# The start-up of a one-core kernel: broadcast weights, an unbroken warm-up, and work moved between engines

## The chip, the cores and the metric

The kernel runs on one core of a Trainium2 chip. The metric is the device time of one execution in microseconds (us). The profile shows when each step of the start-up begins, to a hundredth of a microsecond.

The engines are TensorE (PE in the profile; PEld is its weight load), VectorE (DVE), ScalarE (ACT), GpSimd (POOL) and SyncE (SP, which only issues DMAs here).

## The reference

```python
# x: (8, 4096, 192) float32, weight: (8, 7), w_in: (192, 2048), w_out: (2048, 192), beta: (2048,)
w = exp(weight - weight.max(-1)); w = w / (w.sum(-1) + 1e-9)       # softmax over 7 taps, for each of 8 heads
y[b, s, h, g] = sum_k w[h, k] * x_pad[b, s + k, h, g]              # causal convolution, pad of 6
hid = y @ w_in                                                     # (32768, 2048)
out = (hid * sigmoid(beta * hid)) @ w_out                          # (32768, 192), float32
```

## The kernel before

The work is cut into 32 stages of 1024 tokens. A stage has 16 blocks of 128 hidden columns. A block is six matmuls into a PSUM tile `ph`, one SiLU on ScalarE that writes `g`, and "pairs" of output matmuls for earlier blocks. The convolution of later stages runs on VectorE. In stage 0 two thirds of the 192 columns run on TensorE, each third as seven matmuls with diagonal matrices `diag`, since nothing else is ready then; the last third is split between TensorE and VectorE. "Chunk 1's convolution" below is the first third of stage 1, done on TensorE from block 4 of stage 0 on. The change touches only the start-up and stage 0.

```python
    nc.scalar.dma_start(out=cw8, in_=weight)                 # 8 x 7, one row for each head
    load_x(x0, 0); load_x(x1, TOK); ...                      # SyncE's queue: x0, x1, w_out, ...
    load_w_in(0)                                             # GpSimd's queue, casts to bf16 on the way
    # softmax: exponential on 8 partitions, spread to 128 by a small matmul with a 0/1 matrix
    nc.vector.reduce_max(nmax, cw8, ...)
    nc.scalar.activation(e8[:, 0:K], cw8, AF.Exp, bias=nmax, accum_out=e8[:, K:K+1])
    nc.scalar.activation(warm, warm, AF.Silu)                # brings in ScalarE's SiLU table (1.28 us)
    fill(5)                                                  # matmuls on zeros, only to keep TensorE busy
    nc.tensor.matmul(pw, sel, e8, ...)                       # the small matmul
    fill(1, 384)
    for b in range(NB):
        cast_rows(nc.vector.tensor_copy, x0b, x0, b)         # x0 to bf16
    nc.vector.reciprocal(rn, pw[:, K:K+1]); nc.vector.tensor_scalar_mul(cw, pw[:, 0:K], rn)
    for b in range(NB):                                      # transposes of x0, evicted by ScalarE
        transposes(pt, x0b, b); nc.scalar.copy(tokens(xt0, b), pt)
        # fills of 256 and 384 columns after b = 0 and 1, then 384 and 256 behind the loop
    ... # diag = identity * cw, on VectorE
    for c in range(NG - 1):                                  # convolution of stage 0 on TensorE
        for k in range(K): diag_tap(k, xt0[:, c], pv[:, 0, :])
        nc.scalar.copy(cts[0][:, c, :], pv[:, 0, :])         # eviction
        for b in range(2): cast_rows(nc.scalar.copy, x1b, x1, 2 * c + b)
    ...
    scale_w_out(0)                                           # w_out times 1/beta, on VectorE
```

(Cuts are marked by `...`.)

## Time and profile before

| | before |
|---|---|
| time, median of the first 4 executions | 692.76 us (692.5 to 693.43) |
| transposes of x0 start | 4.76 us |
| first convolution on TensorE | 7.83 to 10.88 us |
| first SiLU | 14.31 us |
| second block of stage 1 | 33.01 us |
| end of the last eviction (ScalarE, 687.70 + 0.32) | 688.02 us |

After stage 0, TensorE is busy without a gap. These are the busy times by stretch of before: the stretch in us and its length, then busy time (and count) of TensorE, its weight loads, VectorE, ScalarE and GpSimd, the recorded clock, DMA share, GB/s.

```profile
16.40:31.90 15.50, 14.91 (x192) 9.02 (x192) 14.64 (x19) 15.06 (x15) 0.00 (x0) 1.00 0.92 203
31.90:679.00 647.10, 647.08 (x10881) 493.17 (x10881) 499.22 (x421) 551.86 (x496) 0.00 (x0) 1.00 0.35 92
```

TensorE has 0.02 us of idle in 647. With that code left as it is, only its start, its idle before that, and what follows its last matmul can change the total. (The trace of before holds no record of the clock, so the 1.00 in these lines says nothing about it; the step of the matmuls below does.) This is the start, from the timeline of before: start, duration, engine, line, operation, and in brackets the idle before it and what ended it.

```profile
1.26 2.31 PE L228 MATMUL ph<-zeros 128*128 128x512 bf16 x5 [1.26 <-DVE warm L178]
2.23 0.15 DVE L217 TENSOR_REDUCE nmax<-cw 8x1 f32<-8x7 f32 x1 [0.92 <-DMA cw<-in_weight_dram]
4.29 0.74 DVE L233 CAST x0b<-x 128x384 bf16<-128x384 f32 x2 [1.78 <-DMA x<-in_x_dram]
4.76 0.50 PE L240 MATMUL pb<-ident_b,x0b 128*128 128x128 bf16 x3
7.83 3.04 PE L279 MATMUL ph<-xt,diag 128*128 128x512 f32 x7
10.71 1.79 PE L279 MATMUL pb<-xt,diag 128*128 128x512 f32 x7
14.31 16.15 ACT L425 ACTIVATE g<-ph,beta 128x1024 bf16<-128x1024 f32 x15
```

The 8x7 weights are in at 2.2 us, before x0 (4.29). The seven matmuls of the first convolution start 0.43 us apart, those of the second 0.23 us: the step halves on the way, at about 10.5 us, and the text calls this the slow and the fast clock (in a_dve_order below the clock was recorded at 0.51 while the first convolution took 3.55 us). At the end of stage 0, TensorE waits for VectorE's last tap (from the timeline of before; the tap group ends at 29.27 + 2.60 = 31.87). The third line is the last eviction of the kernel:

```profile
29.27 2.60 DVE L335 SCALAR_TENSOR_TENSOR ct<-xt,cw,ct 128x1024 bf16<-128x1024 bf16 x2
31.92 0.61 PE L417 MATMUL ph<-ct,w_in_s 64*128 64x512 bf16 x4 [0.40 <-DVE ct L335]
687.70 0.32 ACT L466 COPY osb<-pa 128x192 f32<-128x192 f32 x1 [1.00 <-PE pa L450]
```

### The profile page before, as it was taken

The numbers are of one execution on the slowest core, as the hardware profiler recorded it, in microseconds if no ns is written. First come the engines' busy times: TensorE is split into PE (matmuls) and PEld (weight loads), VectorE is DVE, ScalarE is ACT, GpSimd is POOL, SyncE is SP. The second block draws the span as 40 slices with busy tenths as digits, with TensorE's granted clock in tenths as the row PEclk, the third lists the DMA queues.
The fourth block names the chain that finished last, engine by engine and source line by source line (L and its number), as shares of the span: only waits on it lengthen the run. The fifth ranks groups of instructions, "written<-read, shape, count | busy, mean of one in ns | idle before, by whom it ended". The sixth has DMA issues, their size and how long they took to land.

```text
span 690.7 us, 24335 instructions
## 1 busy us (share of the span) xinstructions
PE 684.2 (99%) x11311; PEld 518.1 (75%) x11311; DVE 526.6 (76%) x466; ACT 579.1 (84%) x531; POOL 6.8 (1%) x18
## 2 busy tenths in 40 slices
PE   8999999999999999999999999999999999999997
PEld 4677777777777777777777777777777777777776
DVE  6888877797777797777887777887777977777712
ACT  6988888888888888888888888888888888888883
POOL 3000000000000000000000000000000000000000
DMA  9754332344332343332344332443323443322111
GB/s 214 176 117 116 93 104 69 85 116 112 92 104 58 102 116 104 97 95 61 109 116 105 93 83 70 116 116 92 104 56 98 116 106 98 98 60 60 48 37 59
DMA packets 121445, 66.86 MB, mean 97 GB/s; under 512 B 53232, under 2 KB 121344, under 8 KB 121344
## 3 DMA queue, kind: packets, MB, share of 16 engines
q1 hardware_dynamic: 119632, 63.73, 34.7%
q0 software_dynamic: 1664, 1.57, 1.4%
q8 instruction: 88, 1.44, 0.9%
q14 instruction: 13, 0.11, 0.1%
q10 hardware_dynamic: 48, 0.01, 0.0%
HBM read 29.89 MB, written 25.17 MB: 80 GB/s over the span
## 4 chain that ended last, share of the span: by engine, by line
PE 97%; DVE 1%; ACT 1%; issue 0%; ACTq 0%
PE ph L417 47%; PE pa L450 24%; PE pb L450 24%; DVE ct L335 1%; ACT g L425 0%; PE ph L279 0%; ACT x1b L233 0%; DVE w_out_s L313 0%; PE pb L279 0%; PE ph L228 0%; DVE ct L396 0%; DVE xb L106 0%; ACT ct L326 0%; PE pb L240 0%; PE ph L240 0%
## 5 line engine op out<-in xcount | busy, mean ns | idle before, releaser
L425 ACT ACTIVATE g<-ph,beta 128x1024 bf16<-128x1024 f32 x512 | 569.7, 1114 | 95.7 <-PE ph L417 89.6
L450 PEld LDWEIGHTS <-g 64*128 64x128 bf16 x8160 | 367.7, 94 | 106.3 <-ACT g L425 0.7
L417 PE MATMUL ph<-ct,w_in_s 64*128 64x512 bf16 x3072 | 422.8, 376 | 1.3 <-ACT g L425 0.9
L335 DVE SCALAR_TENSOR_TENSOR ct<-xt,cw,ct 128x1536 bf16<-128x1536 bf16 (+2 forms) x190 | 336.6, 1772 | 2.5
L450 PE MATMUL pa<-w_out_s,g 64*128 64x192 bf16 x4112 | 244.2, 243 | 0.6 <-ACT g L425 0.5
L450 PE MATMUL pb<-w_out_s,g 64*128 64x192 bf16 (+1 forms) x4048 | 229.7, 243 | 0.0
L417 PEld LDWEIGHTS <-w_in_s 64*128 64x128 bf16 x3072 | 156.7, 94 | 56.7 <-issue 3.4
L468 DVE TENSOR_REDUCE osb<-pa 128x384 f32<-128x768 f32 x64 | 61.3, 957 | 120.8 <-PE pa L450 119.9
L468 DVE TENSOR_REDUCE osb<-pb 128x384 f32<-128x768 f32 x63 | 60.3, 958 | 28.9 <-PE pb L450 28.8
L106 DVE CAST xb<-xf 128x768 bf16<-128x768 f32 x60 | 40.5, 677 | 0.0
L333 DVE TENSOR_SCALAR ct<-xt,cw 128x1536 bf16<-128x1536 bf16 (+2 forms) x32 | 31.1, 972 | 0.0
L466 ACT COPY osb<-pb 128x192 f32<-128x192 f32 x1 | 0.3, 318 | 6.7 <-PE pb L450 6.7
L228 PE MATMUL ph<-zeros 128*128 128x512 bf16 (+2 forms) x10 | 4.7, 551 | 1.3 <-DVE warm L178 1.3
L210 POOL DMA_DIRECT2D w_in_s<-in_moe_w_in_dram x8 | 5.2, 653 | 0.0
L279 PE MATMUL pb<-xt,diag 64*128 64x512 f32 (+1 forms) x21 | 4.7, 453 | 0.0
L313 DVE TENSOR_TENSOR w_out_s<-w_out_raw,beta_r 128x768 bf16<-128x768 f32 x4 | 3.8, 956 | 0.7 <-DMA w_out_raw<-in_moe_w_out_dram 0.6
L121 DVE COPY xt<-xt 128x18 bf16<-128x18 bf16 x27 | 4.3, 159 | 0.0
L326 ACT CAST ct<-ph 128x512 bf16<-128x512 f32 x1 | 0.6, 586 | 3.3 <-PE ph L279 3.3
L279 PEld LDWEIGHTS pb<-xt,diag 64*128 64x128 f32 (+1 forms) x21 | 2.7, 187 | 0.7
L279 PE MATMUL ph<-xt,diag 128*128 128x512 f32 x7 | 3.0, 603 | 0.1
L233 DVE CAST x0b<-x 128x384 bf16<-128x384 f32 x4 | 1.5, 420 | 2.1 <-DMA x<-in_x_dram 2.1
L228 PEld LDWEIGHTS <-zeros 128*128 128x128 bf16 x10 | 1.2, 133 | 2.1 <-DVE warm L178 1.3
(51 smaller groups left out, 27.7 us busy)
## 6 DMA issues: line engine op xcount, KB each, us to landing
out_dram<-osb SPq DMA_DIRECT2D x127, 192.0 KB, 2.1
xf<-in_x_dram SPq DMA_DIRECT2D x60, 384.0 KB, 4.1
xt<-xb SPq DMA_TRANSPOSE x120, 3.1
x<-in_x_dram SPq DMA_DIRECT2D x4, 384.0 KB, 4.6
w_in_s<-in_moe_w_in_dram POOLq DMA_DIRECT2D x8, 192.0 KB, 9.8
w_out_raw<-in_moe_w_out_dram SPq DMA_DIRECT2D x4, 384.0 KB, 14.6
out_dram<-osb SPq DMA_DIRECT2D x2, 96.0 KB, 1.6
cw<-in_weight_dram ACTq DMA_DIRECT2D x1, 0.2 KB
```

Of the source, the lines that this page charges most:

```text
L106: nc.vector.tensor_copy(xbs[ch][:, :, :, h, :], xfs[ch][:, h].rearrange("q b (p c) -> q b c p", c=NG),)
L121: nc.vector.tensor_copy(dst, last[:, :, HALO + TOK - PAD :])
L210: nc.gpsimd.dma_start(out=w_in_s[r * DG : (r + 1) * DG, :, cols], in_=w_in_v[:, :, cols])
L228: nc.tensor.matmul(pf[:, 0, 0:cols], zeros[:, 0:128], zeros[:, 0:cols], start=True, stop=True)
L279: nc.tensor.matmul(pv, diag[rows, k, :], xt[rows, o : o + TOK], start=(k == k0), stop=(k == K - 1),)
L313: nc.vector.tensor_tensor(w_out_s[:, fcs, :], w_out_raw[:, fcs, :], beta_r[:, fcs].unsqueeze(2).to_broadcast((128, NQ, D)), ALU.mult,)
L333: nc.vector.tensor_scalar_mul(dst, src, scalar)
L335: nc.vector.scalar_tensor_tensor(out=dst, in0=src, scalar=scalar, in1=dst, op0=ALU.mult, op1=ALU.add)
L417: nc.tensor.matmul(ph[:, h, :], w_in_s[rows, j, fc * 128 : (fc + 1) * 128], cts[s][rows, j, :], start=(j == 0), stop=(j == NG - 1),)
L425: nc.scalar.activation(gs[s][:, fc], ph, AF.Silu, scale=beta[:, fc : fc + 1])
L450: nc.tensor.matmul(self.po[:, r, b * D : (b + 1) * D], g[rows, fc, self.h, q * BLK : (q + 1) * BLK], w_out_s[rows, fc, :], start=(self.don ...
L468: nc.vector.tensor_reduce(dst, self.po[:, :, 0 : nb * D].rearrange("p r n -> p n r"), axis=mybir.AxisListType.X, op=ALU.add,)
```

## The change

The intent is a shorter start-up. Its parts:
- The weights are loaded by DMA in broadcast form, one row for each of 128 partitions, so that the softmax needs no TensorE matmul.
- The warm-up fills are one unbroken run of nine, and the fills between the transposes are larger.
- The first 256 columns of w_in come raw over SyncE's queue and are cast by ScalarE, so GpSimd's software queue starts later (first issue at 7.67 us in the changed kernel, 2.17 before).
- Two x1 casts stand before ScalarE's first eviction.
- The first w_out scaling moves to GpSimd.
- Chunk 1's convolution is done in three blocks, not four, and three more output pairs are done in stage 0.

```diff
-    nc.scalar.dma_start(out=cw8, in_=weight)
+    for h in range(2):
+        nc.scalar.dma_start(out=wq[h * DG : (h + 1) * DG, :],
+                            in_=weight.unsqueeze(1).to_broadcast((H, HP, K)))
     load_x(x0, 0)
+    nc.sync.dma_start(out=beta_q, ...)
+    for r in range(2):
+        nc.sync.dma_start(out=w_in_raw[r * DG : (r + 1) * DG], in_=w_in_v[:, :, 0:F0])   # F0 = 256
     load_x(x1, TOK)
-    load_w_in(0)
-    nc.vector.reduce_max(nmax, cw8, ...)
-    nc.scalar.activation(e8[:, 0:K], cw8, AF.Exp, bias=nmax, accum_out=e8[:, K : K + 1])
+    nc.vector.reduce_max(nmax, wq, ...)
+    nc.scalar.activation(cw, wq, AF.Exp, bias=nmax, accum_out=total)
     nc.scalar.activation(warm, warm, AF.Silu)
+    nc.vector.reciprocal(total, total)
+    nc.vector.tensor_scalar_mul(cw, cw, total)
-    fill(5); nc.tensor.matmul(pw, sel, e8, ...); fill(1, 384)
+    fill(9)
     for b in range(NB):
         cast_rows(nc.vector.tensor_copy, x0b, x0, b)
+        if b == 1: diags(0, 2)
+    diags(2, 4); diags(4, K)
     for b in range(NB):
         transposes(pt, x0b, b); nc.scalar.copy(tokens(xt0, b), pt)
-        # fills of 256 and 384 after b = 0 and 1, 384 and 256 behind the loop
+        fill(1, (256, 384, 128, TOK)[b])          # and one of 512 behind the loop
+    nc.scalar.copy(w_in_s[:, :, 0:F0], w_in_raw)
     ...
+        for b in ((0, 1), (2,))[c]: cast_rows(nc.scalar.copy, x1b, x1, b)
         nc.scalar.copy(cts[0][:, c, :], pv[:, 0, :])
-        for b in range(2): cast_rows(nc.scalar.copy, x1b, x1, 2 * c + b)
+    cast_rows(nc.scalar.copy, x1b, x1, NB - 1)
     # scale_w_out(i): (nc.vector if i else nc.gpsimd).tensor_tensor(...)
-    CONV1 = {4: (0, 2), 5: (2, 4), 6: (4, 6), 7: (6, K)};  QUOTA_A = {3: 4, 7: 2};  last quota 8
+    CONV1 = {4: (0, 2), 5: (2, 4), 6: (4, K)};  QUOTA_A = {4: 2, 7: 5};  last quota 10
```

(The diff is cut to its core and some lines are joined. Cut are `+load_w_in(F0, FW)`, which loads the rest of w_in's first quarter later, the removal of the 0/1 matrix from GpSimd, a smaller tile of zeros for the fills, and an earlier warm exponential. The load of beta moves from ScalarE's queue to SyncE's.)

More of the change, by code (lines that the diff above doesn't have):

```diff
@@ L148, in load_w_out @@
         nc.sync.dma_start(out=w_out_raw[:, fcs, :], in_=w_out_v[:, fcs, :])
-    e8 = setup.tile([H, K + 1], FP32)
-    cw8 = setup.tile([H, K], FP32)
+    wq = setup.tile([128, K], FP32)
+    for h in range(2):
+        nc.scalar.dma_start(
+            out=wq[h * DG : (h + 1) * DG, :],
+            in_=weight.unsqueeze(1).to_broadcast((H, HP, K)),
+        )
     beta_q = setup.tile([NF, 128], FP32)
-    nc.scalar.dma_start(out=cw8, in_=weight)
-    nc.scalar.dma_start(out=beta_q, in_=moe_beta.rearrange("(c p) -> c p", p=128))
     def load_x(dst, t0):
@@ L167 @@
     load_x(x0, 0)
+    nc.sync.dma_start(out=beta_q, in_=moe_beta.rearrange("(c p) -> c p", p=128))
+    F0 = 256
+    w_in_raw = setup.tile([128, NG, F0], FP32)
+    for r in range(2):
+        nc.sync.dma_start(
+            out=w_in_raw[r * DG : (r + 1) * DG], in_=w_in_v[:, :, 0:F0]
+        )
     load_x(x1, TOK)
@@ L173 @@
     load(3)
-    zeros = setup.tile([128, TOK], BF16)
+    zeros = setup.tile([128, 128], BF16)
     nc.vector.memset(zeros, 0.0)
@@ L178, with load_w_in @@
     nc.vector.memset(warm, 0.0)
+    nc.scalar.activation(warm, warm, AF.Exp)
     xt0 = setup.tile([128, NG, HALO + TOK], FP32R)
     nc.vector.memset(xt0[:, :, 0:HALO].bitcast(FP32), 0.0)
-    nc.scalar.activation(warm, warm, AF.Exp)
-    sel = setup.tile([H, 2, DG], FP32)
-    nc.gpsimd.memset(sel, 1.0)
-    pattern = [[0, 2], [1, DG]]
-    nc.gpsimd.affine_select(
-        out=sel,
-        in_=sel,
-        compare_op=ALU.is_ge,
-        fill=0.0,
-        base=0,
-        pattern=pattern,
-        channel_multiplier=-HP,
-    )
-    nc.gpsimd.affine_select(
-        out=sel,
-        in_=sel,
-        compare_op=ALU.is_ge,
-        fill=0.0,
-        base=HP - 1,
-        pattern=[[-step, n] for step, n in pattern],
-        channel_multiplier=HP,
-    )
     ident = setup.tile([128, 128], FP32)
     make_identity(nc, ident)
-    def load_w_in(i):
-        cols = slice(i * FW, (i + 1) * FW)
+    def load_w_in(c0, c1):
         for r in range(2):
             nc.gpsimd.dma_start(
-                out=w_in_s[r * DG : (r + 1) * DG, :, cols], in_=w_in_v[:, :, cols]
+                out=w_in_s[r * DG : (r + 1) * DG, :, c0:c1], in_=w_in_v[:, :, c0:c1]
             )
-    load_w_in(0)
-    nmax = setup.tile([H, 1], FP32)
-    nc.vector.reduce_max(nmax, cw8, axis=mybir.AxisListType.X, negate=True)
-    nc.scalar.activation(
-        e8[:, 0:K], cw8, AF.Exp, bias=nmax, accum_out=e8[:, K : K + 1]
-    )
+    nmax = setup.tile([128, 1], FP32)
+    total = setup.tile([128, 1], FP32)
+    cw = consts.tile([128, K], FP32)
+    nc.vector.reduce_max(nmax, wq, axis=mybir.AxisListType.X, negate=True)
+    nc.scalar.activation(cw, wq, AF.Exp, bias=nmax, accum_out=total)
     nc.scalar.activation(warm, warm, AF.Silu)
@@ L226, in fill @@
     def fill(n, cols=TOK):
+        zc = zeros.unsqueeze(1).to_broadcast((128, cols // 128, 128))
         for _ in range(n):
-            nc.tensor.matmul(
-                pf[:, 0, 0:cols], zeros[:, 0:128], zeros[:, 0:cols], start=True, stop=True
-            )
+            nc.tensor.matmul(pf[:, 0, 0:cols], zeros, zc, start=True, stop=True)
     def cast_rows(copy, xb, x, b):
@@ L246, in tokens, with diags @@
         return xt[:, :, t : t + 2 * BLK].rearrange("p c (q b) -> p c b q", b=2)[:, :, b % 2]
+    nc.vector.reciprocal(total, total)
+    nc.vector.tensor_scalar_mul(cw, cw, total)
     beta = consts.tile([128, NF], FP32)
     beta_r = setup.tile([128, NF], FP32)
-    cw = consts.tile([128, K], FP32)
-    rn = setup.tile([128, 1], FP32)
-    fill(5)
-    pc = in_a()
-    pw, pb = pc[:, 0, 0 : K + 1], pc[:, 1, 0:NF]
-    nc.tensor.matmul(
-        pw, sel.rearrange("i h p -> i (h p)"), e8, start=True, stop=True
-    )
-    fill(1, 384)
+    diag = setup.tile([128, K, 128], FP32R)
+    def diags(k0, k1):
+        nc.vector.tensor_tensor(
+            diag[:, k0:k1],
+            ident.unsqueeze(1).to_broadcast((128, k1 - k0, 128)),
+            cw[:, k0:k1].unsqueeze(2).to_broadcast((128, k1 - k0, 128)),
+            ALU.mult,
+        )
+    fill(9)
     for b in range(NB):
         cast_rows(nc.vector.tensor_copy, x0b, x0, b)
-    nc.vector.reciprocal(rn, pw[:, K : K + 1])
-    nc.vector.tensor_scalar_mul(cw, pw[:, 0:K], rn)
+        if b == 1:
+            diags(0, 2)
+    diags(2, 4)
+    diags(4, K)
     hold = setup.tile([1, 1], BF16)
     nc.gpsimd.tensor_copy(hold, x0b[0:1, 0, 0, 0, 0:1])
+    load_w_in(F0, FW)
     for i in range(1, NW):
-        load_w_in(i)
-    diag = setup.tile([128, K, 128], FP32R)
+        load_w_in(i * FW, (i + 1) * FW)
     xt1 = setup.tile([128, HALO + TOK], FP32R)
@@ L294 @@
         nc.scalar.copy(tokens(xt0, b), pt)
-        if b == 0:
-            fill(1, 256)
-        elif b == 1:
-            fill(1, 384)
-    fill(1, 384)
+        fill(1, (256, 384, 128, TOK)[b])
+    pb = in_a()[:, 0, 0:NF]
     nc.tensor.transpose(pb, beta_q, ident[0:NF, 0:NF])
     nc.scalar.copy(beta, pb)
-    fill(1, 256)
-    for k0, k1 in ((0, 3), (3, K)):
-        nc.vector.tensor_tensor(
-            diag[:, k0:k1],
-            ident.unsqueeze(1).to_broadcast((128, k1 - k0, 128)),
-            cw[:, k0:k1].unsqueeze(2).to_broadcast((128, k1 - k0, 128)),
-            ALU.mult,
-        )
+    fill(1)
+    nc.scalar.copy(w_in_s[:, :, 0:F0], w_in_raw)
     def scale_w_out(i):
         fcs = slice(i * NQ, (i + 1) * NQ)
-        nc.vector.tensor_tensor(
+        (nc.vector if i else nc.gpsimd).tensor_tensor(
             w_out_s[:, fcs, :],
@@ L325 @@
             diag_tap(k, xt0[:, c], pv[:, 0, :])
+        for b in ((0, 1), (2,))[c]:
+            cast_rows(nc.scalar.copy, x1b, x1, b)
         nc.scalar.copy(cts[0][:, c, :], pv[:, 0, :])
-        for b in range(2):
-            cast_rows(nc.scalar.copy, x1b, x1, 2 * c + b)
+    cast_rows(nc.scalar.copy, x1b, x1, NB - 1)
     def tap(dst, src, k):
@@ L377, in second @@
         nc.vector.tensor_copy(xt1[:, HALO - PAD :], xt[:, 0, HALO - PAD :])
-    CONV1 = {4: (0, 2), 5: (2, 4), 6: (4, 6), 7: (6, K)}
+    CONV1 = {4: (0, 2), 5: (2, 4), 6: (4, K)}
     conv1_ps = []
@@ L523 @@
         5: [None],
-        7: [conv1_evac, lambda: scale_w_out(2), lambda: rows_of(2), None],
+        6: [conv1_evac, lambda: scale_w_out(2), lambda: rows_of(2), None],
         8: [None, lambda: scale_w_out(3)],
@@ L528 @@
     }
-    QUOTA_A = {3: 4, 7: 2}
+    QUOTA_A = {4: 2, 7: 5}
     queue = deque()
@@ L545 @@
             elif u > 7:
-                output(s, u, 5 if u < NF - 1 else 8, "ab")
+                output(s, u, 5 if u < NF - 1 else 10, "ab")
             elif u in QUOTA_A:
```

## The prediction

> **What bounds the kernel now.** Busy time by stretch: from 31.9 to 679.0 us of the 690.7 us span TensorE is busy 647.08 of 647.1 us. A block of hidden columns costs 1.31 us there (starts 33.01, 34.32, 35.63 in the timeline), ScalarE's SiLU only 1.11. The change leaves that code alone, so only the first 32 us and TensorE's idle in it can move. There the chain of waits runs:
> - Warm-up and transposes to 7.8 us.
> - First convolution 7.83-10.88: seven matmuls, 0.43 us from start to start; from about 10.5 us the step is 0.23.
> - ScalarE 10.90-14.31: two evictions (0.59, 0.58) and four casts (0.66 each) in a row. First SiLU at 14.31.
> - Stage 0: 16 SiLUs at 1.08 us. TensorE idles 0.75 us before 15.47.
> - VectorE without a gap 22.33-31.88, ending in taps which TensorE waits for (resumes 31.92).
>
> **What the change does.**
> 1. Warm-up. Nine fills (0.43 us cold, estimate 3.9) run from about 1.1 to 5.0 us, and larger fills stand between the transposes. [...] after the broken warm-up the step halves only at 10.5 us, after 2.7 us of dense convolution. I give 65% that convolution 0 is already fast: 7 x 0.23 = 1.6 instead of 3.0 us.
> 2. ScalarE order. It gains a 128x768 cast of w_in (estimate 0.9 us from 0.59 for 512 columns), but two x1 casts now precede the first eviction and run under the convolution. From the beta copy's end at about 7.7: 0.9 + 4 x 0.66 + 2 x 0.58 = 4.7, plus handover: first SiLU at 12.8 us (13.9 if the clock is late), 1.5 earlier.
> 3. DMA. Before, x1's second half lands 8.3 us after issue, at about 10.6, sharing the engines with w_in's software queue. That queue now starts later, and x1 should land by 8.5 although 0.39 MB of raw w_in goes ahead of it.
> 4. Softmax. No TensorE matmul; the weights should land by about 3.3 us and cw be ready near 4.3, when x lands. x0 casts stay about where they are (4.3 to 6.1-6.6).
> 5. VectorE. The first w_out scaling (0.96 us) goes to GpSimd, removing a 0.62 us DMA wait; the second-chunk evictions (15.33 before) start near 13.1. Chunk 1's convolution ends one block earlier. So VectorE's last tap ends near 29.8 instead of 31.88. The GpSimd scaling should [...] be ready for the first output matmul, now at block 4.
> 6. Quotas: 52 instead of 49 output pairs in stage 0: at 0.082 us a pair, 0.25 us.
>
> **Sum.** TensorE resumes for stage 1 about 2.0 us earlier with 0.25 less left: 2.2 us if warm, about 1.1 if not. Everything after is the same dense sequence. I predict 691.0 us, 690.1 to 692.3. Faster by 2% would need 13.9 us out of a start-up of 32, so within 2% is all but certain.
>
> **What would show it.** Step of the first convolution's matmuls 0.23 us; first SiLU 12.5-13.2; x1 casts before the first eviction without a DMA wait; VectorE's taps ending near 30; TensorE's idle at stage 1's start under 0.8 us; 1.31 us a block afterwards.
>
> **What would make it wrong.** The clock stays slow through the first convolution; the weights land late, so that VectorE, in order, holds the x0 casts; x1 or raw w_in lands after 9 us; the GpSimd scaling ends after 17 us and the first output matmul waits; [...] or ScalarE's earlier finish is lost because TensorE's stage-0 work (about 15.5 us) is already the limit.

## The result

| | before | changed |
|---|---|---|
| time, median | 692.76 us (692.5 to 693.43, 4 runs) | 694.21 us (694.13 to 694.78, 4 runs) |
| x0 casts start (VectorE) | 4.29 | 6.95 |
| transposes start (TensorE) | 4.76 | 7.41 |
| first convolution, duration of the seven matmuls | 3.04 (from 7.83) | 3.52 (from 10.15) |
| first SiLU | 14.31 | 17.04 |
| end of the last eviction | 688.02 | 690.07 (689.75 + 0.32) |

The ratio is 1.0021, with a 95% interval of 1.0004 to 1.0039. The changed kernel is slower by 1.4 us, inside the 2% band, but outside the predicted 690.1 to 692.3.

These lines of the timeline after answer to those of before:

```profile
0.74 1.85 ACTq L153 DMA_DIRECT2D wq<-in_weight_dram  x2
0.99 4.02 PE L216 MATMUL ph<-zeros 128*128 128x512 bf16 x9 [0.99 <-DVE warm L188]
6.00 0.16 DVE L205 TENSOR_REDUCE nmax<-wq 128x1 f32<-128x7 f32 x1 [4.96 <-DMA wq<-in_weight_dram]
6.95 0.73 DVE L219 CAST x0b<-x 128x384 bf16<-128x384 f32 x2
7.41 0.50 PE L226 MATMUL pb<-ident_b,x0b 128*128 128x128 bf16 x3 [2.40 <-DVE x0b L219]
10.15 3.52 PE L272 MATMUL ph<-xt,diag 128*128 128x512 f32 x7
13.49 1.79 PE L272 MATMUL pb<-xt,diag 128*128 128x512 f32 x7
17.04 5.17 ACT L410 ACTIVATE g<-ph,beta 128x1024 bf16<-128x1024 f32 x5 [0.52 <-PE ph L402]
689.75 0.32 ACT L451 COPY osb<-pa 128x192 f32<-128x192 f32 x1 [1.00 <-PE pa L435]
```

VectorE waits 4.96 us for the broadcast weights and can only then cast x0. TensorE finishes its nine fills at 5.01 us and idles 2.40 us. The chain of waits of the changed kernel says the same (start, length, what):

```profile
0.74 1.21 ACTq L153
1.98 3.92 DMA wq<-in_weight_dram
6.00 0.17 DVE nmax L205
6.19 0.40 ACT cw L206 x2
6.61 0.17 DVE total L234
6.81 0.23 DVE cw L235
7.04 0.33 DVE x0b L219
```

The first convolution is as slow as before (0.43 us a matmul). So two things went otherwise than predicted: the weights landed at 5.9 us and not at 3.3, and the clock did not rise before the convolution. What follows separates them, and then values the remaining parts.

The profiled execution is the slowest of the four (694.78 us; the others took 694.13 to 694.27). Its mean recorded clock is 1.000 and theirs is 0.997: in those three the clock must have been recorded at a lower speed for a while, about 4 us if at half (an estimate: 0.003 of 693 us, doubled), probably after a first rise, as in a_dve_order below (0.51 there). No trace of them is kept, so what is said of the changed kernel's clock holds for one execution.

### The profile page after: what moved, and what is told of

It is laid out like the page before. It is cut to its first block, busy times and chain, and to the rows that moved or that the text cites. A ratio compares the mean times of both kernels' runs of the same rounds, so it can differ in the third digit from the quotient of the medians.

```text
span 693.0 us, 24340 instructions
## 1 busy us (share of the span) xinstructions
PE 684.8 (99%) x11313; PEld 521.7 (75%) x11313; DVE 522.7 (75%) x466; ACT 580.0 (84%) x532; POOL 7.5 (1%) x16
## 4 chain that ended last, share of the span: by engine, by line
PE 98%; ACT 1%; DMA 1%; ACTq 0%; DVE 0%; issue 0%; DVEq 0%
PE ph L402 48%; PE pa L435 25%; PE pb L435 24%; ACT g L410 1%; DMA wq<-in_weight_dram 1%; PE pb L272 0%; PE ph L272 0%; PE ph L216 0%; ACTq L153 0%; PE pb L226 0%; PE ph L226 0%; PE pa L272 0%; ACT cw L206 0%; DVE x0b L219 0%; ACT osb L451 0%
## 5 line engine op out<-in xcount | busy, mean ns | idle before, releaser
L402 PEld LDWEIGHTS <-w_in_s 64*128 64x128 bf16 x3072 | 158.9, 94 | 55.4 <-issue 2.9
L216 PE MATMUL ph<-zeros 128*128 128x512 bf16 (+3 forms) x14 | 6.5, 585 | 1.0 <-DVE warm L188 1.0
```

Source lines behind the costliest of these rows:

```text
L216: nc.tensor.matmul(pf[:, 0, 0:cols], zeros, zc, start=True, stop=True)
L402: nc.tensor.matmul(ph[:, h, :], w_in_s[rows, j, fc * 128 : (fc + 1) * 128], cts[s][rows, j, :], start=(j == 0), stop=(j == NG - 1),)
```

## The experiments

Twelve kernels ran, in three jobs of four. Each job has its own executions of the kernel before, with medians of 692.80, 693.17 and 692.85 us, so kernels of different jobs are best compared by their ratio to before. All gave correct results. Names starting with `a_` are built on the changed kernel, `b_` on the kernel before, `te_` on `a_te_softmax`.

| kernel | median us (runs) | ratio to before, 95% interval | first convolution (us) | first SiLU (us) |
|---|---|---|---|---|
| changed | 694.21 (4) | 1.0021, 1.0004 to 1.0039 | 3.52 | 17.04 |
| a_dve_order | 695.3 (5) | 1.0033, 1.0021 to 1.0046 | 3.55 | 17.23 |
| a_both_order | 692.33 (5) | 0.9988, 0.9975 to 1.0 | 1.87 | 13.94 |
| a_te_softmax | 691.71 (5) | 0.9982, 0.997 to 0.9995 | 1.86 | 13.30 |
| b_dma_softmax | 699.65 (4) | 1.0091, 1.0076 to 1.0107 | 3.35 | 20.97 |
| a_long_fill | 693.2 (5) | 1.0, 0.9986 to 1.0013 | 1.87 | 15.19 |
| a_weights_first | 693.67 (4) | 1.0007, 0.9993 to 1.0021 | 2.22 | 14.91 |
| te_old_fills | 693.02 (5) | 1.0, 0.9988 to 1.0013 | 3.23 | 14.39 |
| te_evict_first | 692.0 (5) | 0.9985, 0.9973 to 0.9998 | 1.86 | 13.46 |
| te_w_in_pool | 693.65 (5) | 1.0011, 0.9999 to 1.0024 | 1.86 | 14.81 |
| te_dve_scale | 692.16 (5) | 0.9991, 0.9978 to 1.0003 | 1.86 | 13.49 |
| te_old_quota | 692.5 (5) | 0.9994, 0.998 to 1.0008 | 1.86 | 13.17 |
| b_new_fills | 692.71 (5) | 0.9997, 0.9985 to 1.001 | 1.87 | 13.61 |

The column on the first convolution is the duration of its seven-matmul group in the timeline; about 1.86 is the fast clock throughout, 3.0 and more the slow one. In a_weights_first (2.22) the last fill before it still took 0.61 us, as in the changed kernel, where in a_te_softmax it took 0.39; so the step changed at the start of the seven.

### Is it the order on VectorE? (a_dve_order)

```diff
-    nc.vector.reduce_max(nmax, wq, ...); nc.scalar.activation(cw, wq, AF.Exp, ...); SiLU table; normalise
     for b in range(NB):
         cast_rows(nc.vector.tensor_copy, x0b, x0, b)
-        if b == 1: diags(0, 2)
+    nc.vector.reduce_max(nmax, wq, ...); nc.scalar.activation(cw, wq, AF.Exp, ...); SiLU table; normalise
+    diags(0, 2)
     diags(2, 4); diags(4, K)
```

> The changed kernel with one move on VectorE: the four x0 casts now come before the softmax and the diagonals, so VectorE no longer waits for the broadcast weights (landed at 5.9 us) with x0 already there (4.3). Theory A (the loss is VectorE's order alone: in-order VectorE holds the casts 2.65 us): x0 casts start at 4.3, the first convolution near 8, time 691.9 to 692.5 us. Rival B (ScalarE is in order too: the evictions of the transposes stand behind the exponential and a 1.28 us table load, so they still start at about 8.0 us): the casts start at 4.3, but the first eviction stays at 7.9 to 8.2 us and the time stays at 694.2 within 0.3.

The x0 casts started at 4.17 us, but the time did not fall: 695.3 us, with runs from 694.25 to 696.78 (the changed kernel had 694.13 to 694.78). This is 1.1 us above what rival B expected, and that excess stays unexplained. ScalarE's part of the timeline of a_dve_order shows why nothing was gained:

```profile
6.28 0.30 ACT L248 ACTIVATE cw<-wq,nmax 128x7 f32<-128x7 f32 x1 [2.16 <-DVE nmax L247]
6.69 1.28 ACT L249 ACT_TABLE_LOAD   x1
7.98 0.20 ACT L249 ACTIVATE warm<-warm 8x1 f32<-8x1 f32 x1
8.09 0.47 ACT L286 CAST xt<-pb 128x384 fp32r<-128x384 bf16 x1
8.62 0.48 PE L223 MATMUL pb<-ident_b,x0b 128*128 128x128 bf16 x3 [3.14 <-ACT xt L286]
```

The first transposes were done early (from 4.64 us), but their eviction stands in ScalarE's program behind the exponential, which waits for the weights, and behind a 1.28 us table load. It starts at 8.09, against 8.00 in the changed kernel, and TensorE waits 3.14 us for it (the last line above is TensorE's). So rival B holds in its mechanism: here a late input blocks each engine that has it in its program (VectorE's casts at 6.95 us in the changed kernel, ScalarE's eviction at 8.09 here), and freeing one of two gained nothing.

This run also shows the clock fall again. These are the busy times by stretch of a_dve_order; the third figure from the end is the recorded clock:

```profile
3.50:7.00 3.50, 1.75 (x12) 0.80 (x11) 1.85 (x7) 1.31 (x5) 2.35 (x5) 1.00 0.98 227
7.00:10.50 3.50, 1.89 (x11) 1.24 (x11) 1.77 (x5) 3.16 (x8) 3.02 (x5) 0.51 1.01 294
```

In this execution the clock was recorded up at about 3.7 us, during the fills (trace record). After a stretch in which TensorE was busy for half the time (1.75 of 3.50 us), it was back at half speed (0.51), and the first convolution took 3.55 us.

### Both orders (a_both_order)

```diff
     for b in range(NB):
         transposes(pt, x0b, b); nc.scalar.copy(tokens(xt0, b), pt)
+        if b == 1: reduce_max; exponential; normalise; diags(0, 2); diags(2, 4); diags(4, K)
         fill(1, (256, 384, 128, TOK)[b])
+    nc.scalar.activation(warm, warm, AF.Silu)     # the table load, now behind the four evictions
```

> As a_dve_order, and on ScalarE the exponential goes behind the second eviction and the SiLU table load behind the fourth. Both theories: x0 casts and evictions start when x0 lands, transposes near 5.0 us, first convolution near 8 us instead of 10.7. ScalarE then has 1.5 us of table load and dummy between the evictions and the w_in cast. If the wait for the weights is the whole loss: 692.0 to 692.9 us, that is 1.3 to 2.2 below the changed kernel. If the loss lies elsewhere (GpSimd scaling, quotas, w_in cast): 693.8 or more although the convolution starts at 8.

```profile
7.79 1.87 PE L263 MATMUL ph<-xt,diag 128*128 128x512 f32 x7 [0.31 <-DVE diag L237]
```

Measured: 692.33 us, first convolution from 7.79 us, as both theories said. The weights are just as late here (their last packets move at 5.50 us and VectorE reads them at 6.15), but nothing stands behind them that could have run before. And the first convolution took 1.87 us: with TensorE fed almost without a pause (busy for 3.40 of the 3.50 us from 3.50 on), the clock was up in time (trace record: at 5.76 us). So the wait for the weights, together with what it does to the clock, is the loss of the changed kernel, up to the 0.6 us by which this median lies above that of a_te_softmax below; the runs of the two overlap.

### The old softmax in the changed kernel (a_te_softmax), the new one in the old kernel (b_dma_softmax)

```diff
 a_te_softmax, against the changed kernel:
-    wq = ...; two broadcast loads; softmax on 128 partitions
+    8x7 load; exponential on 8 partitions; fill(5); small matmul; fill(3); reciprocal and scale behind the x0 casts
 b_dma_softmax, against the kernel before:
-    8x7 load; exponential on 8 partitions; small matmul; reciprocal and scale behind the x0 casts
+    two broadcast loads; softmax on 128 partitions; reciprocal and scale in front of the x0 casts
```

> The changed kernel with the softmax of before (8x7 load, exponential on 8 partitions, small TensorE matmul that spreads it), all other parts of the change kept, fills 5 + 3. If the late broadcast weights are the whole loss, the first convolution starts at 8.0 to 8.3 us and the time is 691.5 to 692.8. If the rest of the change gains what was predicted (first SiLU at 12.8, needs the fast clock in the first convolution): 691.0 or less. If the rest gains nothing because TensorE's first convolution is still at 0.43 us a matmul: first SiLU at 14.3 to 14.7, time 692.3 to 692.9, as before.

> The kernel before with only the softmax changed to broadcast weights by DMA. If the broadcast causes the loss by itself: x0 casts start at about 6.5 to 7 us instead of 4.3, first convolution 2.3 to 2.7 us later, time 695.0 to 695.6 us. If the loss comes from other parts of the change: within 0.4 us of before (692.8).

a_te_softmax took 691.71 us, 0.18% below before and the lowest ratio (te_evict_first, at 0.9985, is level with it). Its first expectation holds; the second, 691.0 or less with the first SiLU at 12.8, does not, so with the wait removed the rest of the change still gains less than was predicted. b_dma_softmax took 699.65, 6.9 us above before, where 2.3 to 2.7 had been expected: the direction was right, the size was not. There w_in's software queue starts early (first issue at 1.43 us, 7.67 in the changed kernel) and shares the DMA engines with the weights too (in before it took 32.3% of the 16 engines' time in the first 12 us). That this is the reason was not tested apart, but the wait of its chain is twice as long:

```profile
2.04 7.91 DMA wq<-in_weight_dram
```

The 28-byte packets in the trace show the same. The one 8-row load of before moved at 1.77 to 1.87 us. The two broadcast loads moved at 3.18 to 3.86 and 4.70 to 5.26 us in the changed kernel, and at 3.17 to 4.12 and 6.03 to 9.43 us in b_dma_softmax.

These are the lines of a_te_softmax's timeline that answer to those above:

```profile
2.19 0.15 DVE L223 TENSOR_REDUCE nmax<-cw 8x1 f32<-8x7 f32 x1 [1.08 <-DMA cw<-in_weight_dram]
4.43 0.74 DVE L239 CAST x0b<-x 128x384 bf16<-128x384 f32 x2 [1.94 <-DMA x<-in_x_dram]
5.11 0.53 PE L246 MATMUL pb<-ident_b,x0b 128*128 128x128 bf16 x3
8.07 1.86 PE L297 MATMUL ph<-xt,diag 128*128 128x512 f32 x7
13.30 4.14 ACT L434 ACTIVATE g<-ph,beta 128x1024 bf16<-128x1024 f32 x4 [0.52 <-PE ph L426]
28.24 2.60 DVE L344 SCALAR_TENSOR_TENSOR ct<-xt,cw,ct 128x1024 bf16<-128x1024 bf16 x2
686.42 0.32 ACT L475 COPY osb<-pa 128x192 f32<-128x192 f32 x1 [1.00 <-PE pa L459]
```

The first SiLU is 1.01 us earlier than before (13.30 against 14.31), VectorE's last tap ends 1.03 us earlier (30.84 against 31.87), the second block of stage 1 starts 1.03 us earlier (31.98 against 33.01), and the last eviction ends 1.28 us earlier (686.42 + 0.32 = 686.74 against 688.02). The last quarter microsecond fits the three output pairs that were moved into stage 0 (three times 0.082 us; in before, eight pairs start within 0.66 us, 300.39 to 301.05). The span of this profile, 690.6 us, hardly shows it, because it happened to end 3.8 us after the last eviction, where before it was 2.7; the other four executions had spans of 689.8 to 690.1.

### Why are the weights late? (a_weights_first)

```diff
-        nc.scalar.dma_start(out=wq[...], in_=weight.unsqueeze(1).to_broadcast((H, HP, K)))
+        nc.sync.dma_start(out=wq[...], in_=weight.unsqueeze(1).to_broadcast((H, HP, K)))   # ahead of x0
```

> The changed kernel with the two broadcast loads on SyncE's queue ahead of x0, so that they move before any large load is on the way. Theory A (the broadcast loads are late because their small packets stand in line behind x0's on the same engines): the weights land by 3.3 us (their issue ends near 2.6), x0 lands 1.9 us later, near 6.2, and the x0 casts start then. Rival B (a broadcast load is that slow by itself): the weights still land near 5.5 to 6 us. The time is 0 to 1 us below the changed kernel with A, the same or more with B.

```profile
4.13 0.16 DVE L205 TENSOR_REDUCE nmax<-wq 128x1 f32<-128x7 f32 x1 [3.09 <-DMA wq<-in_weight_dram]
```

VectorE read the weights at 4.1 us instead of 6.0, though not at 3.3. Their packets moved at 2.26 to 2.85 and 2.96 to 3.68 us. So up to 1.9 us of the lateness came from the traffic that was ahead of them, as theory A has it (0.37 us of it is an earlier end of the issue on the other queue, 2.22 against 2.59 us). The edit changes two things at once, the queue and the place ahead of x0, and no run separates them. About 0.8 us against its 3.3 is left and was not taken apart: a broadcast load also takes longer to issue (0.61 to 1.21 us for each in the changed kernel, against 0.60 for the single 8-row load). The time, 693.67, gains less than the weights do, since x0 is now behind them (x0 casts at 5.64 us).

### Does the clock matter by itself? (a_long_fill, te_old_fills)

```diff
 a_long_fill, against the changed kernel:
-    fill(9)
+    fill(15)
 te_old_fills, against a_te_softmax:
-    fill(3)                                  # after the small matmul
+    fill(1, 384)
-        fill(1, (256, 384, 128, TOK)[b])     # and fill(1) behind
+        # 256 and 384 after b = 0 and 1; 384 and 256 behind the loop, as before
```

> The changed kernel with 15 fills in place of 9: they end at about 7.4 us cold, or 5.5 if the clock rises, and bridge the 2.4 us in which TensorE idles for the late x0 casts. Theory A (part of the loss is a second one: the late casts also break the warm-up, so the first convolution is slow): the first convolution runs at 0.24 us a matmul, first SiLU near 15.9 instead of 17.04, time 0.7 to 1.3 us below the changed kernel (693.0 to 693.6). Rival B: the clock in the convolution costs nothing, since ScalarE's casts bound the first SiLU: step 0.24, time 694.0 to 694.4.

> a_te_softmax with only the fills of before (5, then 384 columns, and 256 / 384 / none / 384 / 256 between the transposes). In a_te_softmax the first convolution ran at 0.24 us a matmul, before at 0.43. Theory A (the fills make the clock rise before the convolution): here the first convolution falls back to about 0.43 us a matmul, 1.2 us longer, first SiLU 14.0 to 14.4 instead of 13.30, time 692.3 to 692.9. Rival B (the clock's rise is a matter of the phase of each run): the step is 0.24 here too and the time is 691.4 to 692.0.

Both support theory A. In a_long_fill the weights and the x0 casts are as late as in the changed kernel (casts at 6.81 us), and only the pause is filled:

```profile
0.99 5.43 PE L216 MATMUL ph<-zeros 128*128 128x512 bf16 x15 [0.99 <-DVE warm L188]
7.27 0.34 PE L226 MATMUL pb<-ident_b,x0b 128*128 128x128 bf16 x3 [0.84 <-DVE x0b L219]
9.94 1.87 PE L272 MATMUL ph<-xt,diag 128*128 128x512 f32 x7
```

The first convolution ran fast, the first SiLU came 1.85 us earlier than in the changed kernel, and the time fell from 1.0021 to 1.0 of before, about 1.5 us (1.0 us by the medians). In te_old_fills, where nothing but the fills was taken back, the first convolution fell back to 3.23 us and the whole gain of a_te_softmax was gone (1.0 against 0.9982).

```profile
7.79 3.23 PE L297 MATMUL ph<-xt,diag 128*128 128x512 f32 x7
```

One profile each would not rule out its rival B, the phase of the run, but the clock records of all profiles do so fairly well. In a_dve_order the record changes after 3.41 us and again after 6.83, twice that. In te_old_fills the clock was recorded up at 10.78 us; if its record moves in the same steps of 3.41 (my estimate, from a_dve_order alone), one step earlier is 7.37, where it had not risen. te_evict_first and te_dve_scale have nearly this phase (up at 7.31 and 7.55) and the new fills, and rose a step earlier. All six profiles with fills 5 and 3 rose between 4.82 and 7.55 us, before the convolution; in a_te_softmax, where transposes and fills alternated almost without a pause from 5.11 us to the convolution, it was at 7.09.

In the profile of te_old_fills the last eviction ended at 687.42, 0.68 us later than in a_te_softmax; the times differ by 1.3. The profile's figure is the smaller and comes from one execution each, so the fills are worth 0.7 to 1.3 us.

### What are the other parts worth? (te_evict_first, te_w_in_pool, te_dve_scale, te_old_quota, b_new_fills)

Each of the first four takes back one part in a_te_softmax. The last puts only the new fills into the kernel before.

```diff
 te_evict_first:  eviction, two x1 casts, eviction, two x1 casts (the order of before)
 te_w_in_pool:    no raw load and no cast; the first quarter of w_in on GpSimd's queue, early
 te_dve_scale:    -(nc.vector if i else nc.gpsimd).tensor_tensor(   +nc.vector.tensor_tensor(
 te_old_quota:    CONV1 and the last quota of before; QUOTA_A = {4: 4, 7: 2} (before: {3: 4, 7: 2}); chunk 1's eviction after block 7
 b_new_fills:     before, with fill(5), small matmul, fill(3), and 256 / 384 / 128 / 512 / 512
```

> a_te_softmax with only the order of before on ScalarE after the w_in cast: eviction, two x1 casts, eviction, two x1 casts. If the casts' new place is what lets the first SiLU come early: the four casts and the second eviction stand in a row after the first convolution, first SiLU near 13.9 to 14.2 instead of 13.30 and time 0.4 to 0.8 us longer (692.1 to 692.6). If stage 0 is bound by TensorE anyway: first SiLU later, time within 0.3 us of a_te_softmax (691.7).

The new order of casts and evictions is worth little or nothing: 692.0 against 691.71 with overlapping runs (691.76 to 692.8 against 691.51 to 692.32), first SiLU at 13.46 against 13.30, last eviction at the same time within 0.03 us. In te_evict_first the first SiLU follows ScalarE's casts at once; in a_te_softmax ScalarE is done earlier, and then waits 0.52 us for TensorE, so that most of what the new order frees is lost.

> a_te_softmax with w_in's first quarter loaded as before, early on GpSimd's queue, and without the raw load and ScalarE's cast. If the raw load is worth its place (it frees the engines for x1): x1's second half lands 2 us later and the time is 0.3 us or more longer than a_te_softmax (691.7). If it is worth nothing: within 0.3 us, since ScalarE loses a 0.83 us cast.

Taking the raw load back costs about 2 us, more than any other part (1.0011 against 0.9982). Without it x1 and w_out land later than in a_te_softmax, and both ScalarE and VectorE wait. From the waits of te_w_in_pool in its first 36 us (engine, what, waited for, total us, times, longest), and its timeline:

```profile
ACT x1b L235 <- DMA x<-in_x_dram: 3.4, 2, 2.9
20.29 0.96 DVE L315 TENSOR_TENSOR w_out_s<-w_out_raw,beta_r 128x768 bf16<-128x768 f32 x1 [1.33 <-DMA w_out_raw<-in_moe_w_out_dram]
```

The longest time from issue to landing of x0 and x1 is 9.8 us here and 5.9 us in a_te_softmax. Since the issues moved too, the times from the start say more (landing records of the traces, in us):

| landed at | before | a_te_softmax | te_w_in_pool |
|---|---|---|---|
| x1, first half | 6.94 | 9.18 | 10.35 |
| x1, second half | 10.67 | 10.24 | 12.63 |
| w_out, second quarter | 18.21 | 14.66 | 20.26 |

So te_w_in_pool does not have the loads of before: they land 2.0 to 3.4 us later. It keeps beta's load on SyncE's queue ahead of x1, whose issue therefore starts at 2.33 us, behind the first w_in load (2.17), where before it started at 1.83. The 2 us are thus the raw load's worth with beta's load in its new place; against the loads of before the raw load was not run, and b_new_fills below, with those loads and the fast clock, took 692.71 us against 693.65.

One more thing shows here. A VectorE copy of 18 elements in each partition took 1.08 us (17.00 to 18.08) where before it took 0.16, while GpSimd's scaling ran from 16.59 to 18.06. Whether the one slowed the other was not tested.

> a_te_softmax with the first w_out scaling on VectorE again. VectorE's chain grows by 0.96 us plus a wait for w_out of up to 0.6. If VectorE's last tap still bounds the start of stage 1: TensorE waits there again, time 0.5 to 1.2 us longer. If stage 0 is bound by TensorE's own work (as the trace of a_te_softmax says, VectorE's last tap at 30.8 with TensorE resuming at once): within 0.4 us of 691.7.

692.16 us, with runs of 691.59 to 693.09. VectorE's last tap ended at 30.50 us, even earlier than with the scaling on GpSimd (30.84), and so did the last eviction (686.52 against 686.74). The median lies 0.46 us above 691.7, just outside the second expectation's 0.4, but the traces are on its side: moving the scaling to GpSimd is no gain that these runs can tell from none.

> a_te_softmax with the quotas of before (49 instead of 52 output pairs in stage 0) and chunk 1's convolution spread over four blocks. 3 pairs move to the end, and VectorE's taps start one block later: 0.25 us from the pairs if TensorE is busy all through stage 0 (then nothing is gained by moving them, and the times agree within 0.3), or up to 1 us longer if VectorE's later taps make TensorE wait at stage 1.

692.5 us, 0.8 us slower by the medians (0.9994 against 0.9982). VectorE waited 1.8 us for chunk 1's convolution (0.9 in a_te_softmax), and TensorE then waited for VectorE's taps, which ended at 31.16 us. The last eviction ended at 687.31, 0.57 later. The quotas and the convolution in three blocks together give 0.6 to 0.8 us.

> The kernel before with only the fills of the changed kernel (5 + 3 around the small softmax matmul, then 256 / 384 / 128 / 512 / 512); all else as before. te_old_fills came out at 693.0, level with before, so if the fills are the whole gain of a_te_softmax this kernel takes 691.6 to 692.1 us with the first convolution at 0.24 us a matmul and the first SiLU near 13.1 to 13.5. If the fills need the other parts (x1 landing early, casts before the eviction) the first SiLU stays at 13.9 or later and the time at 692.4 or more.

692.71 us, level with before, although the first convolution ran fast and the first SiLU came at 13.61 instead of 14.31. The time is that of the second alternative (692.4 or more), but not for its reason, a late first SiLU. The chain of waits shows what took the gain: VectorE's scaling waits for w_out, and the rest of VectorE's stage 0 follows that.

```profile
2.86 11.72 DMA w_out_raw<-in_moe_w_out_dram
14.68 0.96 DVE w_out_s L309
15.63 1.87 DVE xt L366 x4
```

VectorE's last tap ended at 32.09 us, no earlier than before (31.87). Here the fast clock alone did not pay, since w_out landed no earlier (its first quarter at 14.58 us, 14.36 before), and by the times the other parts without it did not pay either. Neither alone beats the kernel before: te_old_fills is at 1.0, b_new_fills at 0.9997, both together at 0.9982. Which of the other parts the fast clock needs was not tested one by one.

## Why the prediction was wrong

- **What bounds the kernel: right.** The stretch after stage 0 kept its 1.31 us a block; the difference of 2.05 us between the last evictions of the two profiles arises in the first 35 us (the second block of stage 1 starts 2.29 us later, and 0.25 us of pairs is saved at the end).
- **Step 4 (softmax) failed.** It said that "the weights should land by about 3.3 us and cw be ready near 4.3, when x lands. x0 casts stay about where they are". The weights landed at 5.9 us, cw was ready at about 7.0, and the x0 casts moved from 4.29 to 6.95. I had taken the landing of the small 8-row load and added issue time. But a broadcast has 64 rows in each of two loads, takes longer to issue (0.61 to 1.21 us for each against 0.60), and meets x0's traffic, which the small load slipped in ahead of (packets at 1.77 us against 3.18 to 5.26). In a_weights_first up to 1.9 us of the delay went with the move ahead of that traffic. The sentence on what would make it wrong had this very case; I gave it too little weight. I also named only VectorE as blocked; a_dve_order showed that ScalarE blocks just as well (first eviction at 8.09 us).
- **Step 1 (warm-up): that the fills can bring the fast step was right, the outcome failed as a consequence of step 4.** The nine fills ended at 5.01 us as estimated (5.0), but x0 was not there, TensorE paused 2.40 us, and in the profiled execution the convolution ran at 0.43 us a matmul. With the weights early (a_te_softmax) or the pause filled (a_long_fill) the step is 0.23 to 0.24 us, as predicted.
- **Step 2 (ScalarE): mis-sized.** With the weights out of the way the first SiLU came at 13.30 us, not 12.8, and the new order has little part in it (te_evict_first: 13.46).
- **Step 3 (DMA): the landing of x1 failed; w_out gained instead.** It said that "x1 should land by 8.5". In a_te_softmax x1's second half landed at 10.24 us, hardly before the 10.67 of before. The longest time from issue to landing did fall, from 8.3 us to 5.9, but mostly because the issue starts later (4.3 against 2.35 us). What came earlier is w_out (second quarter at 14.66 us, 18.21 before). The prediction did not give the loads a term of their own; te_w_in_pool loses about 2 us, with the limit named there.
- **Step 5 (VectorE): mis-sized.** In a_te_softmax the last tap ended at 30.84 us, not 29.8. The scaling on GpSimd took 1.47 us (0.96 on VectorE; the profile's spans on GpSimd are rough) and was ready in time, but VectorE then waited 0.89 us for chunk 1's convolution instead (0.61 before). te_dve_scale is no slower beyond its scatter.
- **Step 6 (quotas): right** for the three pairs, 0.25 us at the end (1.28 less 1.03). The rest of what te_old_quota lost is put down to the convolution in three blocks; no run separates the two.
- **The sum.** Predicted 2.2 us gained, or 1.1 with the slow clock. Without the broadcast softmax the change gains 1.1 us by the medians (691.71 against 692.80), 1.28 by the last eviction. With it, about 2.5 us are lost again (694.21 less 691.71; medians of two jobs): about 1.0 to 1.5 are the broken warm-up (a_long_fill) and the rest, by subtraction, the later start.

Open: why a broadcast load still needs until 4.1 us with no traffic ahead, why b_dma_softmax lost 6.9 us and not 2.5, and how the clock went in the executions without a kept trace.

## What to carry to other kernels

In a start-up, ask of every new load which instructions stand behind its first reader on that engine, and on the engines that read the result; put work whose input is there first in front of it, on all of them. Here the small load moved ahead of the big ones (packets at 1.77 us), and the broadcast loads, which take longer to issue (0.61 to 1.21 us for each against 0.60), fell behind them and waited (packets at 3.18 to 5.26 us). Compare landings as times from the start: a shorter time from issue to landing can be little but a later issue (the longest fell from 8.3 to 5.9 us in a_te_softmax, while x1's second half landed at 10.24 us against 10.67). A warm-up is only as good as its end: if the fills stop before the first real matmul is ready, they can be lost, so size them by the latest arrival and look at the step of the first real matmuls in the trace. How long they had to be varied here: in the profiled execution of the changed kernel 4.02 us of unbroken fills all ran slowly and, with 2.40 us of idle behind, left nothing for the convolution (0.43 us a matmul); in a_long_fill 5.43 us of them were enough in the profiled execution even with 0.84 us of idle behind; in a_dve_order the clock was recorded up about 2.7 us after the first fill.
